# One accumulating DMA over all 4608 elements of three tap pairs, and four transpose groups for every chunk

## The chip, the cores and the metric

The kernel runs on one core of a Trainium2 chip. The metric is the device time of a run in microseconds (us).

## The reference, cut to what matters

```
# x: (8, 4096, 192), weight_gen: (8, 4096, 8 heads, 7 taps), w_in: (192, 2048), w_out: (2048, 192)
w = softmax(weight_gen, axis=taps)
y[b, s, head, g] = sum over k of w[b, s, head, k] * x_padded[b, s + k, head, g]   # 7 taps, 6 zeros in front
h = y.reshape(32768, 192) @ w_in
out = (h - tanh(h)) @ w_out
```

## The kernel before

The kernel goes through 32 blocks of 1024 tokens. For each block POOL multiplies x by the weights of one tap at a time (seven products of 128 x 1536). Taps 0 and 1, 2 and 3, 4 and 5 are pairs: one product goes to `even`, the other to `odd`, and a DMA issued from POOL adds `odd` into `even`. The first three blocks (PLAIN) do without that DMA.

```
ACC = NPAIR * J * D - J * R          # 3*8*192 - 8*64 = 4608 - 512 = 4096 elements a partition
...
            if k == K - 2 and in_pairs:
                nc.gpsimd.dma_start(
                    out=even[:].rearrange("p i c j h g -> p (i c j h g)")[:, 0:ACC],
                    in_=odd[:].rearrange("p i c j h g -> p (i c j h g)")[:, 0:ACC],
                    accum_op=mybir.AluOpType.add,
                    max_dma_last_dim=4096,
                )
```

PE then sums the products and turns them to channels first in one go: `conv`, the "transposes" or "the stage" below, multiplies each 64 x 128 piece by a unit matrix and adds up in PSUM. The 512 elements that the DMA leaves out belong to the third chunk of 64 channels, so that chunk gets `odd` as a fifth group.

The order of a block on PE is eight times (12 first-layer matmuls, 32 second-layer ones), with the next block's stage behind the seventh:

```
    for n in range(NTOT):
        if n + 3 < NTOT:
            load_wg(n + 3)
            load_x(n + 3)
        for p in range(J):
            gemm1(n, 2 * p)
            gemm1(n, 2 * p + 1)
            ...
                gemm2((n - 1) * J + p)
            ...
                if p == (6 if n > 0 else 7):
                    conv(n + 1, (0, 1))
                if p == (6 if n > 1 else 7):
                    conv(n + 1, (2,))
```

The softmax here doesn't subtract the row's maximum and nothing guards it: scores larger than these inputs give would overflow.

## Time and profile before

| | before |
|---|---|
| median time | 770.6 us (770.07 to 770.72) |
| PE busy, share of the span | 736.7 us, 96% |
| POOL busy | 695.2 us, 90% |
| PE's distance from stage to stage, middle of the run | 22.63 us |
| POOL's distance from issue to issue of the DMA | 22.64 us |

Two parts of the page: the queues (packets, megabytes, share of 16 engines' span), and two groups (busy us, mean ns of one, idle time before and who ended it).

```profile
q0 software_dynamic: 10816, 31.99, 25.8%
q8 instruction: 115, 1.88, 1.0%
...
L233 PE MATMUL pc<-ident,odd 64*128 64x64 bf16 x448 | 15.5, 198 | 13.1 <-DVE odd L192 12.8
L201 POOL DMA_DIRECT2D even<-odd x29 | 34.9, 1205 | 9.1 <-POOL odd L192 9.1
```

The idle 13.1 us before the odd matmuls are nearly all (12.8) in the first blocks, where VectorE makes products; the pair blocks have none.

### The profile page before, as it was taken

What the parts mean: (1) busy time and instruction counts of PE and PEld (TensorE: products, weight loads), DVE (VectorE), ACT (ScalarE), POOL (GpSimd) and SP (SyncE); (2) the same over time, 40 slices, a digit from 0 to 9 for tenths busy, and PEclk for the clock granted to TensorE, in tenths of its full rate; (3) what the DMA queues carried; (4) which work ended last, traced back from release to release, by engine and by line L of the source; (5) the groups of instructions that cost most, each with busy time, mean ns of one, the idle gap of its engine ahead of it and who ended that gap; (6) DMA issues with size and microseconds to landing.
All of it is one profiled execution on the core that took longest, in us unless ns stands there. A gap on an engine that the chain in (4) does not pass through costs nothing.

```text
span 768.7 us, 32330 instructions
## 1 busy us (share of the span) xinstructions
PE 736.7 (96%) x14784; PEld 583.1 (76%) x14784; DVE 652.9 (85%) x595; ACT 640.8 (83%) x865; POOL 695.2 (90%) x290
## 2 busy tenths in 40 slices
PE   2799999999999999999999999999999999999997
PEld 2377787777777777788777777777778777787777
DVE  5987888888898888889888888888888988888883
ACT  1777878888888888888888888888888888888883
POOL 5999999999999999999999999999999999999100
PEclk9999999999999999999999999999999999999999
DMA  7823776555677555577655557765556765542412
GB/s 209 184 81 87 182 181 150 118 145 147 169 182 174 131 129 148 150 180 182 164 123 133 150 160 182 180 128 137 143 150 172 182 181 115 125 142 72 98 43 84
DMA packets 25847, 111.37 MB, mean 145 GB/s; under 512 B 4800, under 2 KB 9456, under 8 KB 21624
## 3 DMA queue, kind: packets, MB, share of 16 engines
q1 hardware_dynamic: 14688, 76.95, 29.9%
q0 software_dynamic: 10816, 31.99, 25.8%
q8 instruction: 115, 1.88, 1.0%
q10 hardware_dynamic: 208, 0.39, 0.2%
q14 instruction: 20, 0.16, 0.1%
HBM read 54.49 MB, written 25.17 MB: 104 GB/s over the span
## 4 chain that ended last, share of the span: by engine, by line
PE 93%; DVE 2%; issue 1%; POOL 1%; DMA 1%; ACT 1%; SPq 0%; POOLq 0%
PE ph L257 43%; PE obank L289 43%; PE pc L233 6%; DVE gt L269 2%; PE po L323 1%; DMA x_t<-in_x_dram 1%; POOL even L192 1%; ACT th L267 0%; ACT convT L244 0%; POOL odd L192 0%; DVE zr L151 0%; DVE zsum L145 0%; SPq L117 0%; SPq L93 0%; SPq L121 0%
## 5 line engine op out<-in xcount | busy, mean ns | idle before, releaser
L269 DVE TENSOR_TENSOR gt<-ph,th 128x1024 bf16<-128x1024 f32 x512 | 602.8, 1219 | 93.3 <-ACT th L267 92.7
L267 ACT ACTIVATE th<-ph 128x1024 f32<-128x1024 f32 x512 | 497.2, 1022 | 65.7 <-PE ph L257 64.9
L257 PE MATMUL ph<-convT,w_in 64*128 64x512 bf16 x3072 | 382.1, 378 | 7.5 <-DVE gt L269 5.0
L289 PEld LDWEIGHTS <-gt 64*128 64x128 bf16 x7936 | 345.1, 94 | 53.4 <-issue 2.5
L289 PE MATMUL obank<-w_out,gt 64*128 64x192 bf16 x7936 | 374.6, 243 | 2.9 <-issue 2.1
L192 POOL TENSOR_TENSOR even<-x_t,wsm 128x1536 bf16<-128x1536 f32 x94 | 272.8, 2903 | 3.9 <-DMA x_t<-in_x_dram 1.6
L192 POOL TENSOR_TENSOR odd<-x_t,wsm 128x1536 bf16<-128x1536 f32 x93 | 269.9, 2903 | 0.0
L257 PEld LDWEIGHTS <-w_in 64*128 64x128 bf16 x3072 | 180.1, 94 | 108.4 <-issue 11.8
L192 POOL TENSOR_TENSOR last<-x_t,wsm 128x1536 bf16<-128x1536 f32 x31 | 103.4, 3336 | 0.0
L307 ACT ACTIVATE out_sb<-obank 128x192 f32<-128x192 f32 x248 | 81.9, 330 | 10.5 <-PE obank L289 4.6
L244 ACT ACTIVATE convT<-pc 128x1024 bf16<-128x1024 f32 x64 | 48.9, 808 | 31.6 <-PE pc L233 31.5
L233 PE MATMUL pc<-ident,even 64*128 64x64 bf16 x2304 | 47.9, 192 | 2.9 <-POOL even L192 1.5
L233 PEld LDWEIGHTS <-even 64*128 64x128 bf16 x2304 | 42.7, 96 | 4.1 <-issue 2.2
L201 POOL DMA_DIRECT2D even<-odd x29 | 34.9, 1205 | 9.1 <-POOL odd L192 9.1
L163 POOL TENSOR_TENSOR wsm<-e_t,zr 128x448 f32<-128x448 f32 x30 | 41.7, 1390 | 0.0
L233 PE MATMUL pc<-ident,odd 64*128 64x64 bf16 x448 | 15.5, 198 | 13.1 <-DVE odd L192 12.8
L135 ACT ACTIVATE e_t<-wg_t 128x448 f32<-128x448 f32 x32 | 18.5, 578 | 8.2 <-DMA wg_t<-in_weight_gen_dram 8.2
L233 PE MATMUL pc<-ident,last 64*128 64x64 bf16 x768 | 23.3, 192 | 1.8 <-issue 1.7
L145 DVE TENSOR_REDUCE zsum<-e_t 128x64 f32<-128x448 f32 x32 | 19.5, 609 | 2.9 <-ACT e_t L135 2.9
L233 PEld LDWEIGHTS <-odd 64*128 64x128 bf16 x448 | 11.3, 100 | 13.6 <-DVE odd L192 12.9
L151 DVE RECIPROCAL zr<-zsum 128x64 f32<-128x64 f32 x30 | 16.6, 553 | 3.0
L233 PEld LDWEIGHTS <-last 64*128 64x128 bf16 x768 | 17.0, 96 | 2.2 <-issue 1.8
(20 smaller groups left out, 48.7 us busy)
## 6 DMA issues: line engine op xcount, KB each, us to landing
x_t<-in_x_dram SPq DMA_DIRECT2D x24, 1344.0 KB
even<-odd POOLq DMA_DIRECT2D x29, 1024.0 KB, 8.8
out_dram<-out_sb SPq DMA_DIRECT2D x31, 768.0 KB
x_t<-in_x_dram SPq DMA_DIRECT2D x8, 1176.0 KB
wg_t<-in_weight_gen_dram SPq DMA_DIRECT2D x32, 224.0 KB
x_t<-in_x_dram SPq DMA_DIRECT2D x8, 157.5 KB
w_in<-in_moe_w_in_dram POOLq DMA_DIRECT2D x6, 128.0 KB, 7.5
w_out<-in_moe_w_out_dram POOLq DMA_DIRECT2D x1, 768.0 KB, 10.8
```

The costliest lines, as they stand in the source:

```text
L135: nc.scalar.activation(out=e_t[:].rearrange("p j h k -> p (j h k)"), in_=wg_t[:].rearrange("p j h k -> p (j h k)"), func=ACT.Exp,)
L145: nc.vector.reduce_sum(out=zsum[:], in_=e_t[:].rearrange("p j h k -> p (j h) k"), axis=AX.X)
L163: return eng.tensor_mul(wsm.rearrange("p j h k -> p (j h) k"), e_t[:].rearrange("p j h k -> p (j h) k"), zr.rearrange("p (n o) -> p n o", ...
L192: eng.tensor_mul(dst[k].rearrange("p c j h g -> p j h c g"), x_t[:, k : k + J, :].rearrange("p j (h c g) -> p j h c g", h=H, c=NC), w[:, : ...
L201: nc.gpsimd.dma_start(out=even[:].rearrange("p i c j h g -> p (i c j h g)")[:, 0:ACC], in_=odd[:].rearrange("p i c j h g -> p (i c j h g)" ...
L233: nc.tensor.matmul(pc[:, r, col : col + R], lhsT=prods[c][gi][r * R : (r + 1) * R, c, 2 * j : 2 * j + 2].rearrange("p j h g -> p (j h g)") ...
L244: nc.scalar.activation(out=convT[:, c0 : c0 + nch, :].rearrange("p c (j r t) -> p r (c j) t", r=2, t=R), in_=pc[:, :, 0 : nch * JH * R].re ...
L257: nc.tensor.matmul(ph[:, r, :], lhsT=w_in[r * R : (r + 1) * R, c, f * P : (f + 1) * P], rhs=convT[r * R : (r + 1) * R, c, :], start=(c == ...
L267: last_act[0] = nc.scalar.activation(out=th[:], in_=ph_f, func=ACT.Tanh)
L269: last_sub[0] = nc.vector.tensor_sub(gt[:], ph_f, th[:])
L289: mm = nc.tensor.matmul(po[:, 0:D], lhsT=g_of[n][f][r * R : (r + 1) * R, col : col + P], rhs=w_out[r * R : (r + 1) * R, f, :], start=(r == ...
L307: last_act[0] = nc.scalar.activation(out=out_sb[:, j, :], in_=po[:, 0:D], func=ACT.Copy)
```

## The change

The intent is to rid PE, the busiest engine, of eight matmuls a block by letting the DMA add the last 512 elements too. The DMA then has three pieces of 1536 elements a partition.

```
-    ACC = NPAIR * J * D - J * R
...
-                    out=even[:].rearrange("p i c j h g -> p (i c j h g)")[:, 0:ACC],
-                    in_=odd[:].rearrange("p i c j h g -> p (i c j h g)")[:, 0:ACC],
+                    out=even[:].rearrange("p i c j h g -> p i (c j h g)"),
+                    in_=odd[:].rearrange("p i c j h g -> p i (c j h g)"),
...
-            groups = [even[:, i] for i in range(NPAIR)] + [last[:]]
-            prods_of[n] = [
-                groups + ([odd[:, NPAIR - 1]] if c == NC - 1 else []) for c in range(NC)
-            ]
+            prods_of[n] = [[even[:, i] for i in range(NPAIR)] + [last[:]]] * NC
```

## The prediction

> **What bounds the kernel now.** I read the page first: its busy table, the slices, then the chain that ended last.
>
> ```profile
> PE 736.7 (96%) x14784; PEld 583.1 (76%) x14784; DVE 652.9 (85%) x595; ACT 640.8 (83%) x865; POOL 695.2 (90%) x290
> ...
> PE   2799999999999999999999999999999999999997
> ...
> POOL 5999999999999999999999999999999999999100
> PEclk9999999999999999999999999999999999999999
> ...
> PE 93%; DVE 2%; issue 1%; POOL 1%; DMA 1%; ACT 1%; SPq 0%; POOLq 0%
> ```
>
> The reader is to see two full rows: PE in every slice after the first two, POOL until its work runs out near 715 us. The chain goes through PE for 93% of the span, so PE sets the end, and the clock is full. But POOL has no hole either, so the second question is how far POOL is from setting the pace. Next, the timeline of PE at one transpose stage in the middle.
>
> ```profile
> 409.10 0.88 PE L233 MATMUL pc<-ident,even 64*128 64x64 bf16 x48
> 409.80 0.41 PE L233 MATMUL pc<-ident,last 64*128 64x64 bf16 x16
> 410.03 0.53 PE L233 MATMUL pc<-ident,even 64*128 64x64 bf16 x24
> 410.38 0.30 PE L233 MATMUL pc<-ident,last 64*128 64x64 bf16 x8
> 410.50 0.30 PE L233 MATMUL pc<-ident,odd 64*128 64x64 bf16 x8
> 410.81 1.47 PE L257 MATMUL ph<-convT,w_in 64*128 64x512 bf16 x12
> ```
>
> Columns are start and duration in us. The stage has 104 matmuls; the eight on odd are the fifth group that only the third chunk has. No idle note stands on any row. The stage begins again at 431.73, so a block takes PE 431.73 - 409.10 = 22.63 us, and the stretch view gives 22.61 us of PE busy in it. Then the timeline of POOL in the same block, and far earlier at the load of w_out and at a block without an accumulating DMA.
>
> ```profile
> 29.16 1.23 POOL L350 DMA_DIRECT2D w_out<-in_moe_w_out_dram  x1
> 30.41 2.92 POOL L192 TENSOR_TENSOR odd<-x_t,wsm 128x1536 bf16<-128x1536 f32 x1
> ...
> 57.20 0.97 POOL L163 TENSOR_TENSOR wsm<-e_t,zr 128x448 f32<-128x448 f32 x1
> ...
> 415.45 1.20 POOL L201 DMA_DIRECT2D even<-odd  x1 [0.30 <-POOL odd L192]
> 416.22 3.37 POOL L192 TENSOR_TENSOR last<-x_t,wsm 128x1536 bf16<-128x1536 f32 x1
> 419.09 1.42 POOL L163 TENSOR_TENSOR wsm<-e_t,zr 128x448 f32<-128x448 f32 x1
> ...
> 438.09 1.20 POOL L201 DMA_DIRECT2D even<-odd  x1 [0.30 <-POOL odd L192]
> ```
>
> From issue to issue POOL takes 438.09 - 415.45 = 22.64 us and waits only for itself. PE's 22.63 and POOL's 22.64 are level: this kernel is tuned to where the two meet. PE does not feel it because POOL runs ahead. The last two views are the waits, and the landing time of the DMA.
>
> ```profile
> PE pc L233 <- POOL even L192: 1.5, 2, 1.1
> ...
> even<-odd POOLq DMA_DIRECT2D x29, 1024.0 KB, 8.8
> ```
>
> PE waited for POOL's sums 1.5 us in the whole run and never for the DMA. POOL's **lead** is how long the accumulated sums lie ready before the transposes want them, from starts in the two timelines and the 8.8 us: first pair block 88.47 - (75.77 + 8.8) = 3.9 us; last block 727.09 - (710.17 + 8.8) = 8.1 us. It grew in the first few pair blocks, where PE periods are 23 to 25 us, and has been level since.
>
> **What the Trainium skill says.** "DMA: Bandwidth & Descriptors", section "SDMA does more than copy", gives 2048 as the largest element count of the inline adder. So the 4096 contiguous elements of a partition must go as two pieces now, 256 in all. The trace agrees: the software queue shows 10816 packets, and 29 x (256 + 16) leaves 2928, which is what w_out (2048 rows + 16) and six loads of w_in (144 each) fill. The same page, "Anatomy of one DMA", calls descriptor generation "small, variable" and says that many descriptors can be emitted before the incremental cost shows up. The trace half agrees: w_out with 2048 rows of 192 elements held POOL 1.23 us, the accumulating DMA with 256 pieces 1.20 us, w_in with 64 rows 0.6 us; yet w_out does not add, so it may not be the same code. "GPSIMD Engine Reference", section "Instruction dispatch", says that each of POOL's cores goes on to the next instruction when its own share is done. The trace fits: last starts 0.77 us into the 1.20 us of the DMA, and ends 0.5 us later than other products. "TensorE: Matmul & The Clock Gate", "Wait — 56ns, not 53.3ns?", gives N / 2.4 GHz + 2.5 ns a matmul, 29.2 ns for 64 columns; two row halves side by side make that 14.6 ns, and the trace has (409.80 - 409.10) / 48 = 14.6 ns.
>
> **The change, part by part.**
>
> *Removed on PE.* The fifth group goes: 8 matmuls in each of 29 pair blocks, 232 in all. Their room is the distance of two starts, 410.50 - 410.38 = 0.12 us. The tail after the last group (410.81 - 410.50 less 0.12) stays, behind last. All of it is on the path. 29 x 8 x 14.6 ns = 3.4 us. PE's block becomes 22.51 us. PE alone: 770.7 - 3.4 = 767.3 us.
>
> *Added in the DMA.* 4608 elements instead of 4096, as 384 pieces of 3072 bytes instead of 256 of 4096. By bytes the landing grows to 8.8 x 1.125 = 9.9 us, by pieces at most to 8.8 x 1.5 = 13.2 us. I take 9.9, so 1.1 us off the lead. Even 4.4 us would cost 0.5 us at the first pair block, once. DMA share is about 0.6 in mid-run, so the 12% more of this queue finds room.
>
> *Added on POOL.* Same number of instructions. Only the issue can grow, by an amount d per block. What a DMA costs POOL now: a block with it starts even at 80.95 and again at 103.61, 22.66 us; one without starts at 37.18 and 58.25, 21.07 us; so 1.6 us, of which 0.3 is the wait for odd, 0.8 the part before last starts and 0.45 the longer wsm (1.42 against 0.97). If generation goes by partitions, as 64, 128 and 128 partitions at 0.61, 1.20 and 1.23 us suggest, d is 0. If it goes by pieces, 1.20 x 384 / 256 = 1.80 us and d = 0.6.
>
> *Sum.* The last transpose stage starts at the later of PE's own 727.1 - 3.4 = 723.7 and POOL's 719.0 + 1.1 + 29 d; what follows it stays. At d = 0 POOL has 720.1 and 3.6 us to spare: lead falls by 0.13 us a block but is not used up, and the full 3.4 us are kept. d = 0.12 is where POOL takes over, 0.24 where the gain is gone.
>
> **The rivals.**
>
> *POOL becomes the bound.* At d = 0.3 the last stage starts at 728.8, 1.7 us later than now: 772.4 us. At d = 0.6, 737.5, 10.4 later: 781.1 us. For it: POOL's row without holes, the level periods, and that somebody left out just the 512 elements which make pieces of the full 2048, paying on PE for it. Against it: the 1.23 us of w_out with eight times as many rows. A slowdown over 2% (786.1 us) needs d near 0.77, more than by pieces.
>
> *A wait for the DMA takes the place of the matmuls.* If landing goes by pieces, POOL's date is 719.0 + 4.4 = 723.4 with d = 0, just at PE's 723.7; a landing that scatters by 2 us would then give back 1 or 2 us: 768 to 769 us. Against it: bytes should count more than pieces in packets of 3 to 4 KB.
>
> *PE gains nothing,* since the eight lie in the shadow of something else, such as weight loads: 770.7 us. Against it: the rate of 14.6 ns is the same in every group of the stage and PE is never idle there.
>
> **Range and chances.** I give d near 0 about one half (767 to 768 us), d between 0.1 and 0.6 some 40% (768 to 781 us), more than that 10%. The middle of this is 768.5 us, closer to the PE sum than to the mean because the first case is narrow. The range is 765.5 to 783: below, a little more per matmul than I count; above, d = 0.6 with a slower landing. Faster by over 2% (below 755.3 us) would need four times the PE saving: 1%. Within 2%: 90%. Slower by over 2%: 9%.
>
> **What would show each step right or wrong.** PE matmuls should be 14784 - 232 = 14552, none on odd in a pair block, and the stage 0.12 us shorter. The DMA record on POOL tells d: 1.2 us means PE's sum holds, 1.8 us means POOL's chain. The distance between two issues should stay at 22.64 us; if it is 22.8 or more, PE will show waits on even in the transposes, late in the run first. The landing should read near 9.9 us. The prediction is wrong if POOL's issue takes far more than 1.8 us, if pieces of 3072 bytes land slower than by count, or if a block on PE does not fall to 22.51 us although nothing makes it wait.

## More of the kernel before

```
            groups = [even[:, i] for i in range(NPAIR)] + [last[:]]
            prods_of[n] = [
                groups + ([odd[:, NPAIR - 1]] if c == NC - 1 else []) for c in range(NC)
            ]
...
        pcs = [psum_h.tile([P, 2, HT], FP32, name="pc", tag="ph") for _ in parts]   # in conv
...
        ph = psum_h.tile([P, 2, HT], FP32, name="ph", tag="ph")                     # in gemm1
```

Mark the tag: the stage and the first layer (`gemm1`) share three PSUM slots. A first-layer slot comes free when ScalarE has taken the tanh and VectorE has subtracted it (`gt`).

## The result, and the profile after

The changed kernel takes 775.4 us (774.97 to 776.04) against 770.6 us in the same rounds: ratio 1.0064, 95% interval 1.0047 to 1.0081. Ratios here are the mean time of one kernel's fast runs over that of the other's fast runs of the same rounds, so not quite the ratio of the medians. It lies within 2% and inside the range, but on the other side of the kernel before than the 768.5 us foretold.

The page of the changed kernel, the lines that answer to those shown of before:

```profile
PE 735.4 (95%) x14552; PEld 578.7 (75%) x14552; DVE 653.1 (84%) x595; ACT 640.2 (83%) x865; POOL 697.7 (90%) x290
...
q0 software_dynamic: 14528, 35.79, 28.9%
q8 instruction: 114, 1.87, 1.0%
...
PE 79%; DVE 11%; ACT 6%; DMA 2%; issue 2%; POOL 0%; ACTq 0%
...
L200 POOL DMA_DIRECT2D even<-odd x29 | 37.4, 1289 | 9.0 <-POOL odd L191 9.0
...
even<-odd POOLq DMA_DIRECT2D x29, 1152.0 KB, 9.6
```

The 232 matmuls are gone (14784 - 14552). The DMA's issue grew from 1.20 to 1.29 us and its landing from 8.8 to 9.6 us, both near what was foretold. But the chain that ended last is no longer PE alone: VectorE and ScalarE hold 17% of it. (In the kernel before they had 3%, although, as the next lines show, VectorE ended its stages too: the shares alone do not tell.) Now the timeline of one undisturbed stage. PE's rows in the changed kernel, then VectorE's in the same stretch; then VectorE's in the kernel before, which belong to the stage that the prediction shows.

```profile
413.53 0.88 PE L229 MATMUL pc<-ident,even 64*128 64x64 bf16 x48
414.23 0.41 PE L229 MATMUL pc<-ident,last 64*128 64x64 bf16 x16
414.46 0.53 PE L229 MATMUL pc<-ident,even 64*128 64x64 bf16 x24
414.81 0.30 PE L229 MATMUL pc<-ident,last 64*128 64x64 bf16 x8
415.24 1.47 PE L253 MATMUL ph<-convT,w_in 64*128 64x512 bf16 x12
```

```profile
412.83 2.36 DVE L265 TENSOR_TENSOR gt<-ph,th 128x1024 bf16<-128x1024 f32 x2 [0.26 <-ACT th L263]
```

```profile
408.40 2.35 DVE L269 TENSOR_TENSOR gt<-ph,th 128x1024 bf16<-128x1024 f32 x2 [0.26 <-ACT th L267]
```

Changed: the last transposes start at 414.81 and need 8 x 14.6 ns = 0.12 us of room, yet the first layer starts only at 415.24. VectorE's second `gt` ends at 412.83 + 2.36 = 415.19, just ahead of it. Before: VectorE ended at 408.40 + 2.35 = 410.75, and the first layer started at 410.81. So from the start of the stage to the next first-layer matmul both kernels take 1.71 us. The next stage starts at 436.15, and 436.15 - 413.53 is 22.62 us, as before.

That tells why nothing was won. Where the loss came from is in other blocks, such as the stage near 253 us of the changed kernel:

```profile
253.07 0.88 PE L229 MATMUL pc<-ident,even 64*128 64x64 bf16 x48
253.77 0.39 PE L229 MATMUL pc<-ident,last 64*128 64x64 bf16 x15
255.37 0.19 PE L229 MATMUL pc<-ident,last 64*128 64x64 bf16 x1 [1.20 <-issue]
255.38 0.53 PE L229 MATMUL pc<-ident,even 64*128 64x64 bf16 x24
```

PE stops in the middle of a group for 1.2 us (bracketed in the third line). "issue" means that the profile shows nothing that it waited for: no data, no semaphore. These holes can be summed. With stage starts from the timeline, the 28 distances from the first pair block's stage to the last make 727.09 - 88.47 = 638.6 us before and 732.30 - 89.35 = 643.0 us after. Twenty-eight undisturbed blocks are 28 x 22.63 = 633.6 us. I call what is over that the **excess**: 5.0 us before, 9.3 us after. Its growth of 4.3 us is most of the 5.2 us between the two profiled spans (768.7 and 773.9); the other 0.9 us was lost before the first pair block's stage, and both kernels take 41.6 us from the last stage's start to the end.

What the holes wait for shows in their places. In the changed kernel the larger ones inside a stage come at matmul number 1758, 2653, 3548, 4443, 6233, 8023, 8918, 9813, 10708 and 11603, counted through the run. The distances are 895 or 1790. A block has 96 + 96 + 256 = 448 matmuls, so two blocks are 896. In the kernel before they come at 1758, 2653, 3165, 4060 and 8151: distances 895, 512, 895 and 4091. All are multiples of 128, less one for every seven. A matmul has two PE instructions in the trace (weight load and matmul), so 128 of them are 256 instructions; the one that is missing now and then makes room for a semaphore instruction, of which PE has 32. Counted over all PE instructions of the trace, each of these holes stands at a multiple of 256, plus 193. The q8 line gives 16 KB a packet, and 115 packets of 256 instructions would be 29,440, about the 29,603 that PE's trace has. The Trainium skill, "Advanced Engine Details and Errata", section "ISA Cache", says the same: a cache line of 16 KB holds 256 instructions. In the packet records each of these holes ends 2.2 to 2.7 us after the start of the last instruction packet. So PE stops where a new piece of its program begins that has not arrived. The stage runs 192 or 208 instructions in 1.4 or 1.5 us, while elsewhere 256 take some 7.6 us (88 in the 2.61 us of one step of the loop over p), so that is where a late piece hurts.

The packet records also show how late a packet is. Take the moment at which PE enters the piece before. The packet of the first listed hole starts 3.98 us after it in the kernel before and 4.24 us after it in the changed one, and packets of x and `out` keep 15 to 16 of the DMA engines busy meanwhile. Over the pieces that begin in a stage after 100 us the mean is 2.25 us before (23 pieces) and 2.81 us in the changed kernel (16 pieces).

With 448 matmuls a block, 3.5 pieces but for the semaphore instruction, every second stage of the changed kernel meets a new piece at the same place. With 456 the place wanders.

### The profile page after: what moved, and what is told of

It reads as the page before. It is cut to its first block, busy times and chain, and to the rows that moved or that the text cites. A ratio compares the mean times of both kernels' runs of the same rounds, so it can differ in the third digit from the quotient of the medians.

```text
span 773.9 us, 31865 instructions
## 1 busy us (share of the span) xinstructions
PE 735.4 (95%) x14552; PEld 578.7 (75%) x14552; DVE 653.1 (84%) x595; ACT 640.2 (83%) x865; POOL 697.7 (90%) x290
## 4 chain that ended last, share of the span: by engine, by line
PE 79%; DVE 11%; ACT 6%; DMA 2%; issue 2%; POOL 0%; ACTq 0%
PE ph L253 38%; PE obank L285 36%; DVE gt L265 10%; ACT th L263 5%; PE pc L229 2%; PE po L319 1%; DMA w_in<-in_moe_w_in_dram 1%; ACT out_sb L303 1%; DMA w_in<-w_in 0%; DMA wg_t<-in_weight_gen_dram 0%; DVE zsum L144 0%; DVE zr L150 0%; POOL w_in L354 0%; ACT e_t L134 0%; DVE obank L162 0%
## 5 line engine op out<-in xcount | busy, mean ns | idle before, releaser
L303 ACT ACTIVATE out_sb<-obank 128x192 f32<-128x192 f32 x248 | 81.9, 330 | 10.2 <-PE obank L285 4.1
L200 POOL DMA_DIRECT2D even<-odd x29 | 37.4, 1289 | 9.0 <-POOL odd L191 9.0
L229 PE MATMUL pc<-ident,odd 64*128 64x64 bf16 x216 | 6.6, 206 | 13.4 <-DVE odd L191 13.4
L229 PEld LDWEIGHTS <-odd 64*128 64x128 bf16 x216 | 5.4, 105 | 13.6 <-DVE odd L191 13.6
```

What stands on the lines that cost most here:

```text
L200: nc.gpsimd.dma_start(out=even[:].rearrange("p i c j h g -> p i (c j h g)"), in_=odd[:].rearrange("p i c j h g -> p i (c j h g)"), accum_o ...
L229: nc.tensor.matmul(pc[:, r, col : col + R], lhsT=prods[c][gi][r * R : (r + 1) * R, c, 2 * j : 2 * j + 2].rearrange("p j h g -> p (j h g)") ...
L303: last_act[0] = nc.scalar.activation(out=out_sb[:, j, :], in_=po[:, 0:D], func=ACT.Copy)
```

## The experiments

The theories, by the names that the expectations use. **A**: the eight removed matmuls changed where the pieces begin, so the holes come back in every second block. **B**: the longer DMA pushes back the loads behind it, and these or the instruction packets come late. **C**: VectorE's release of a PSUM slot ends the stage. **D**: PE's own matmuls end it. **A2**: the pieces come late because they travel behind the load of x. The packets of that load start 8.6 us ahead of the stage and end 2.6 us ahead (medians) in the kernel before; in the changed one they end 1.9 us ahead. The store of `out` and the load of weight_gen follow x on SP's queue.

The two parts of the change, with x early and late, in one table; the other experiments have their numbers in the text. "Excess" as above, from each profile; "lead" is from the landing of the accumulating DMA to the start of the stage, first and last pair block; the time before is that of the same rounds.

| kernel | DMA elements | groups | load of x | time | before | ratio, 95% | excess | lead |
|---|---|---|---|---|---|---|---|---|
| before | 4096 | 5 | early | 770.6 | | | 5.0 | 3.9, 6.5 |
| changed | 4608 | 4 | early | 775.4 | 770.6 | 1.0064 (1.0047 to 1.0081) | 9.3 | 3.3, 7.2 |
| e1 | 4608 | 5 | early | 773.3 | 770.4 | 1.0034 (1.0017 to 1.0051) | 7.6 | 3.0, 4.8 |
| e2 | 4096 | 4 | early | 771.5 | 770.4 | 1.0014 (0.9999 to 1.0028) | 6.0 | 3.6, 6.6 |
| e6 | 4096 | 5 | late | 765.3 | 770.9 | 0.9924 (0.9909 to 0.9939) | 0.3 | 0.8, 2.4 |
| e9 | 4608 | 5 | late | 766.9 | 770.2 | 0.9958 (0.9943 to 0.9973) | 2.3 | 0.2, 0.2 |
| e10 | 4096 | 4 | late | 766.1 | 770.2 | 0.9948 (0.9933 to 0.9963) | 1.4 | 0.8, 1.1 |
| e5 | 4608 | 4 | late | 770.1 | 770.9 | 0.9987 (0.9970 to 1.0003) | 5.7 | 0.1, 1.2 |

### e1 and e2: one part of the change alone

e1 is the kernel before with the changed DMA, e2 the changed kernel with the DMA of before. Their results are wrong, as 512 sums are counted twice or left out.

```
# e1                                                  # e2
-   out=even[:]....[:, 0:ACC],                        -   out=even[:].rearrange("p i c j h g -> p i (c j h g)"),
+   out=even[:].rearrange("... -> p i (c j h g)"),    +   out=even[:]....[:, 0:ACC],
```

> The DMA of the changed kernel with the five transpose groups of the kernel before (512 sums counted twice, so the result is wrong on purpose). Theory A, PE's instruction stream: the loss comes from the 8 matmuls that are gone, because 896 PE instructions a block are just 3.5 pieces of 256 in the instruction queue, so that the wait for a piece comes back in the transposes of every second block; this kernel has 912 a block again, so it should take 770.6 us give or take 1.5. Rival B, the longer DMA pushes back the loads behind it: 775 us or a little over. In both, POOL's distance from issue to issue is 22.73 us as in the changed kernel.

> The DMA of the kernel before with the four groups of the changed kernel (512 sums left out, wrong on purpose). Theory A: about 775 us, with waits of PE for instructions in the transposes of every second block. Rival B: the DMA is short again, so 770.6 us or less. If both parts count, something between, 772 to 774 us.

Both expectations of theory A fell. The DMA alone costs 2.9 us (773.3 against 770.4) and the groups alone 1.1 us, with an interval that touches 1; together they cost 4.8 us. In both kernels an undisturbed block stays at 22.63 us, and the differences are in the excess (7.6 and 6.0 us). So the new holes come from the DMA more than from the groups, and theory B has the larger part. POOL's distance was 22.74 us in e1 and 22.65 us in e2: the slower issue belongs to the DMA alone.

### e3: fewer matmuls still

The changed kernel without the last tap in the transposes (wrong).

```
-            prods_of[n] = [[even[:, i] for i in range(NPAIR)] + [last[:]]] * NC
+            prods_of[n] = [[even[:, i] for i in range(NPAIR)]] * NC
```

> The changed kernel with the last tap left out of the transposes: three groups, 24 matmuls a block fewer (wrong on purpose). Theory C, the end of the stage is set by VectorE, which frees the PSUM slot that the next first-layer matmul needs: the undisturbed block stays at 22.63 us though 24 x 14.6 ns = 0.35 us of matmuls are gone, and the hole before the next L253 matmul grows from 0.3 to 0.65 us. Rival D, PE's own matmuls set it: the undisturbed block falls to 22.28 us and the run by about 10 us.

This one run took 774.8 us, and the undisturbed block is again 22.63 us, with 72 matmuls in the stage instead of 96 or 104. PE and VectorE in one stage of it:

```profile
412.91 1.23 PE L229 MATMUL pc<-ident,even 64*128 64x64 bf16 x72
414.63 1.47 PE L253 MATMUL ph<-convT,w_in 64*128 64x512 bf16 x12 [0.48 <-DVE gt L265]
```

```profile
412.22 2.36 DVE L265 TENSOR_TENSOR gt<-ph,th 128x1024 bf16<-128x1024 f32 x2 [0.26 <-ACT th L263]
```

The stage ends earlier, the hole behind it grows, and the profile names who ended it: `gt` on VectorE, which ends at 412.22 + 2.36 = 414.58. From the stage's start to the first layer it is 1.72 us, as with 96 and 104. Theory C holds and D falls: transposes of 72 to 104 matmuls (1.05 to 1.52 us at 14.6 ns) lie beside VectorE's work and cost nothing, and the 0.12 us that the change saves lie there too.

### e4 and e11: move where the pieces begin, and nothing else

Both are the changed kernel with 32 idle matmuls, once: e4 before the first transposes, e11 inside the stage of the first pair block, in unused columns of its PSUM tile. The result is right.

```
# e4
+    pad(32)                       # 32 matmuls of ident by ident into a PSUM tile that nobody reads
     conv(0, (0, 1), (2,))
# e11, in conv
+                if n == 3 and gi == 1 and chunks[-1] == NC - 1:
+                    for i in range(32): ...   # ident by ident into columns 256 to 319
```

> The changed kernel with 32 idle matmuls (64 PE instructions, a quarter of a piece) once before the first transposes, where PE has nothing to do; nothing else differs. Theory A: the pieces now end at other places of the transposes, early in the stage of one block and late in the other, so the recurring waits go or shrink: 769 to 773 us. Rival B (DMA): 775 us, unchanged, or the 0.9 us of the added matmuls more.

> The changed kernel, right result, with 32 idle matmuls (64 instructions, a quarter of a piece) once, inside the transposes of the first pair block, so that the start of the run is untouched; e4 had them before the first transposes and lost 4 us there. Theory A: from there on the pieces begin at the places of e4, whose later 28 blocks lost 4.5 us and not 9.3: 770.5 to 772 us. If only the DMA matters: 775.5 to 776 us.

They took 774.2 and 774.2 us (ratios 1.0050 and 1.0052), only about 1 us less than the changed kernel: both missed what theory A gave them (769 to 773 and 770.5 to 772 us). The profiles tell more. In e4 the excess fell from 9.3 to 4.5 us, but the stage of the first pair block began at 92.2 us and not at 89.4, after a hole of 3.8 us in the stage before. In e11 the start was untouched, but the distance from its first pair block to the next grew to 27.5 us, and the excess is 10.2 us in all. Without that first distance it is 5.4 us, against 8.1 us in the changed kernel. So the places of the pieces do decide which stages have holes, and a shift moves them; in these two places it moved a large hole into the first blocks.

### e5 and e6: the load of x behind the stage

The load of x for three blocks on waits for the copy out of the transposes' PSUM. e5 has this edit on the changed kernel, e6 on the kernel before. Both are right in result.

```
             load_wg(n + 3)
-            load_x(n + 3)
...
                     conv(n + 1, (2,))
+                    if n + 3 < NTOT:
+                        load_x(n + 3, behind=last_conv[0])     # a dependency on the copy out of conv's PSUM
```

> The changed kernel, right result; only the load of x for three blocks on is held back until the copy out of the transposes' PSUM, so its 128 rows no longer travel in the 8 us before the stage. Theory A2: PE's instruction pieces queue behind x (and what follows it) on the DMA rings, and PE runs out where the next piece begins inside the fast transposes. Then the recurring holes go, the 28 blocks after the first pair block come close to 28 x 22.63 us, and the run takes 767 to 769 us (POOL's own chain, 22.73 us a block, allows no less than about 767). If x has nothing to do with it: 775 us.

> The same edit to the kernel before, right result. Theory A2: its smaller holes (5.0 us in those 28 blocks) go as well: about 765.5 to 767 us. The gap to the changed kernel with the same edit should shrink from 4.9 to 2 us or less. If x has nothing to do with it: 770.5 us and a gap of 4.9.

e6 took 765.3 us, ratio 0.9924: the fastest of all, clear of both kernels, and as foretold to a few tenths. Its excess is 0.3 us; 26 of its 28 distances are within 0.01 us of 22.63. Its waits have PE's weight loads waiting on "issue" in the transposes (L237) for 1.3 us, where the kernel before (L233) has 4.4 us. First the kernel before, then e6:

```profile
PEld L233 <- issue: 4.4, 7, 1.8
```

```profile
PEld L237 <- issue: 1.3, 3, 0.6
```

So nearly all the excess of the kernel before came with bulk transfers in front of the stage. The edit moves more than x: `out` and weight_gen, which follow it on SP's queue, go with it (the packets of `out` start 14.3 us ahead of a stage and not 4.3), so e6 does not tell x from `out`; no run moves one alone. The Trainium skill, "DMA: Bandwidth & Descriptors", section "Queues, rings and completion order", has each of the 16 engines go round its queues packet by packet, draining several descriptors of one before the next. That would make an instruction packet wait behind x's rows, and the packet records fit it: in e6 the packet of what was the first hole starts within 0.03 us of PE's step into the piece before, and not 3.98 us after it. Over the same 23 pieces the mean falls from 2.25 to 1.29 us. In what order an engine takes its queues no run here shows.

e5 missed: 770.1 us where 767 to 769 was expected, and the gap to e6 did not shrink. But its time goes elsewhere: from its second pair block on a block takes 22.75 us on the mean, POOL's 22.74. Its waits:

```profile
POOL odd L195 <- DMA even<-odd: 3.6, 1, 3.6
PE pc L233 <- DMA even<-odd: 3.2, 2, 2.4
```

The first is a wait of POOL before it may write `odd` of block 4 while the DMA of block 3 still reads `odd`. No kernel with five groups has it (before, e1, e6, e7, e9), and each with four has it once (changed 1.5 us, e2 0.9, e4 1.5, e5 3.6, e8 2.6, e10 2.8, e11 2.6, e12 2.8), as has e3 with three (3.2). With five groups PE reads `odd` last; with four only the DMA does, so the program lets go of it earlier, and the next block is given the buffer that the DMA is just reading. That reading of the allocation is argued; the wait and who has it are shown. It takes 3.6 us of POOL's lead at the start. PE then waits 2.4 us for the DMA of the fifth block, and the lead never recovers (0.1 to 1.2 us).

### e9, e10 and e12: what is left once x is late

e9 and e10 are e1 and e2 with the late load of x (again wrong); e12 is e5 with e11's idle matmuls.

> e1 (long DMA, five groups, wrong on purpose) with the late load of x. With e5, e6 and e10 it makes the square of the two parts once x is out of the way. If the long DMA cost e1 its 2.7 us by pushing x towards the stage, that cost is now gone and only POOL's chain (0.09 us a block and a later landing) can show: 765.5 to 767.5 us, and no recurring holes. If the DMA costs in another way: 768 us or more.

> e2 (short DMA, four groups, wrong on purpose) with the late load of x. If the 896 instructions a block (3.5 pieces) still make a hole in every second block from the other loads, 2 us above e6: 766.5 to 768 us. If x was all there is: as e6, 765.3 us. No kernel of this square should go below e6 by more than 0.5 us, since the undisturbed block is 22.63 us with four groups and with five.

> e5 (changed kernel, late x) with the shift of e11. If alignment and x are two separate contributions, the holes of 0.3 to 0.6 us that e5 still has in every second block shrink: 767.5 to 769 us. What stays is POOL's and the DMA's own date. If they are not: 770 us as e5.

e9 came in as expected; e10's 766.1 us lies between its two forecasts (766.5 to 768, and 765.3). Against their own rounds they gain 3.4 and 4.1 us where e6 gains 5.6, so the long DMA costs 2.3 us with x late and the four groups 1.5 us, near the 2.9 and 1.1 with x early. The cost is not gone, but its kind has changed. In e9 the lead is 0.14 us in eight of 29 blocks, which is the least that PE can have when it waits for the landing: POOL's 22.73 us a block now sets the date. Some holes are left in e9 too, and there the instruction packets wait for the accumulating DMA itself: one starts 3.16 us after PE's step, just as the last packets of that DMA end (3.18 us). In e10 there are small holes and the 2.8 us wait of POOL. In e12 (769.3 us, ratio 0.9990, expected 767.5 to 769 and not told apart from e5) every second stage starts late, as the wait in the first line below shows; the distances alternate between 22.54 and about 22.9 us, mean 22.73, which is POOL's.

```profile
202.84 0.88 PE L243 MATMUL pc<-ident,even 64*128 64x64 bf16 x48 [0.29 <-DMA even<-odd]
203.54 0.41 PE L243 MATMUL pc<-ident,last 64*128 64x64 bf16 x16
203.77 0.53 PE L243 MATMUL pc<-ident,even 64*128 64x64 bf16 x24
204.12 0.30 PE L243 MATMUL pc<-ident,last 64*128 64x64 bf16 x8
204.24 1.65 PE L267 MATMUL ph<-convT,w_in 64*128 64x512 bf16 x12
```

Here the stage starts late, so VectorE has long let go of the slot, and the first layer follows 0.12 us after the start of the last group. In such a stage the removed matmuls do shorten the way to the first layer: it is 1.40 us, and 1.51 us in e9 with five groups. Even there nothing is won, for the next stage comes 22.54 us later in both.

### e7 and e8: an attempt to lift VectorE's date, which failed

If the slots end the stage, using one at a time should help. From the fifth block on the first two chunks' transposes run one pair of f tiles earlier; e7 builds on e6, e8 on e5.

```
-                if p == (6 if n > 0 else 7):
+                if p == (5 if n > 3 else 6 if n > 0 else 7):
                     conv(n + 1, (0, 1))
```

> As e6, and from the fifth block on the transposes of the first two chunks run one pair of f tiles earlier than those of the third, so the stage takes one PSUM slot at a time. Theory C (VectorE's slot ends the stage): the hole before the next L257 matmul goes and an undisturbed block falls from 22.63 to about 22.45 us; POOL (22.64 us) then limits the end: 763 to 766 us. Rival D: 22.63 stays and the time is that of e6.

> As e7 with the changed kernel's DMA and four groups. Theory C: an undisturbed block of about 22.33 us, 0.12 less than e7 because only now the eight matmuls count; but POOL's 22.73 us a block takes over in the last blocks, with waits of PE on even: 766 to 769 us, so not better than e7.

They took 780.4 and 784.4 us (ratios 1.0123 and 1.0176) where 763 to 766 and 766 to 769 were expected, the slowest of all, and a block takes 23.18 us in both. PE in e7:

```profile
412.53 0.30 PE L237 MATMUL pc<-ident,odd 64*128 64x64 bf16 x8
412.78 0.82 PE L261 MATMUL ph<-convT,w_in 64*128 64x512 bf16 x6
413.91 0.82 PE L261 MATMUL ph<-convT,w_in 64*128 64x512 bf16 x6 [0.30 <-DVE gt L273]
```

The second six first-layer matmuls start 1.13 us after the first six, where twelve otherwise take 1.3 us together, and again `gt` lets them go. That is theory C at work once more, but my remedy was wrong: it makes PE meet the wait in a second place. That the block is 23.18 us with five and with four groups fits it.

## Why the prediction was right or wrong

The range and the class were right, but by luck: the room above 770.7 us was there for POOL's issue and for a slow landing, and neither made the loss. The middle had the wrong sign: the sum had 3.4 us of gain and the middle of 768.5 us kept some 2 of them; 4.8 us of loss came. One of the prediction's own signs of being wrong came true: a block on PE did not fall to 22.51 us although no row shows it waiting.

**The failed step** is in "Removed on PE": "The tail after the last group [...] stays, behind last. All of it is on the path." The eight matmuls took the room that was foretold, 0.12 us, but the stage's end is not PE's. The 0.19 us of "tail" that I read off and left unexplained was the wait for `gt` on VectorE, which ended at 410.75, 0.06 us before the first layer began. e3 shows it: 72, 96 or 104 matmuls, 22.63 us. So 29 x 8 x 14.6 ns are worth 0 and not 3.4 us. The rival "PE gains nothing" was right; what I held against it, that PE is never idle there, was read from a column that shows no idle note for so short a hole.

**What was not in the sum at all** is PE's instruction stream. Neither the parts nor the rivals have it, though the page shows its queue. It is where nearly all of the 4.8 us came from: the excess grew by 4.3 us. e1 and e2 put 2.9 us to the DMA and 1.1 us to the groups; together they cost 0.8 us more than the sum, about the spread of such a comparison. e6 shows that in the kernel before these holes go when x, and what follows it, is moved.

**POOL's issue**: d was set at "near 0 about one half", and 0.6 if it goes by pieces. It measured 0.09 us (22.64 to 22.73), the record 1.20 to 1.29 us. Half as many pieces again cost 7% of the issue: the half chance was the right one. POOL did not become the bound of the changed kernel, whose lead is 7.2 us at the end. It did bind in e9 and e12, where PE no longer had holes.

**The landing** was 9.6 us for the 9.9 foretold by bytes. The rival of a wait for the DMA did not come true in the changed kernel (no wait of PE on it); it did in e5, for a reason that I had not seen, the buffer of `odd`. The lead of 8.1 us at the end was read with the median landing; with the landing of the last DMA itself it was 6.5 us.

**Left open**: why the long DMA alone makes the holes larger is shown only in part. e1 has the PE instructions of the kernel before, so its pieces begin at the same places. Of the 23 packets whose piece begins in a stage, 21 start later after PE's step than before, on the mean 2.51 us and not 2.25, and the holes there sum to 6.2 us and not 4.2. In e1 the DMA lands 1.1 us later (9.9 and not 8.8) and x follows it, which fits: the packets of x end 0.4 us closer to the stage (median 2.2 us ahead, not 2.6). That this delay is passed on from x is argued. Nor was it tried why the first blocks lost 0.9 us.

## What to carry to other kernels

Before you count removed work on the busiest engine as gain, look for what ends the stage behind it: a slot that another engine frees at the same moment makes the saving worth nothing. A hole that the profile calls "issue", at distances that are multiples of one instruction piece, was here the engine waiting for its own program; keep bulk transfers out of the microseconds ahead of a stage of many short instructions (here that alone was worth 5.6 us, more than the change moved). And a tile whose last reader goes away is reused earlier: look whether the new order gives you the buffer that a DMA is still reading.

## What the Trainium skill lacked or had wrong

- "Runtime: NRT & Kernel Launch", section "Instruction fetch mechanics", has the next block fetched while the current one runs and calls the cost of crossing a 16 KiB boundary "mostly hidden"; it names a stall only for taken branches. Here straight code stopped too: in the changed kernel ten of the crossings inside a stage left holes of 0.3 to 2.3 us (from start to start), and the excess was 9.3 us.
- Neither that page nor "Advanced Engine Details and Errata", section "ISA Cache", says how a late line looks in a profile: holes marked "issue", each ended 2.2 to 2.7 us after the start of the last instruction packet. No page says that moving bulk transfers can cure it (5.0 to 0.3 us of excess).
- "DMA: Bandwidth & Descriptors" calls descriptor generation "small, variable" without a figure. Here 128 more pieces in an accumulating DMA made its record on POOL 0.08 us longer (1205 to 1289 ns) and POOL's block 0.09 us.
- The same page has no rate for accumulating packets. In the packet records an accumulating piece of 4096 bytes took 374 ns (median) and one of 3072 bytes 282 ns, so about in proportion to bytes, while a plain packet of 6144 bytes took 234 ns.
